# Product 0 of stage one as seven sub-products, taken one batch ahead, from the second expert on

## The chip, the cores and the metric

The kernel runs on 1 core of a Trainium2 chip. The metric is device time in microseconds (us), the median of three runs of one launch. The engines are TensorE (PE; its weight loads are listed as PEld), VectorE (DVE), ScalarE (ACT), GpSimd (POOL) and SyncE (SP), which issues the DMAs.

## The reference, cut to what matters

A block-sparse attention (4 batches, 8 heads, 768 tokens) makes x of 3072 tokens by 512. Then comes a mixture of 8 experts, where every expert sees every token:

```
for e in range(E):                      # 8 experts
    h = np.maximum(x @ w1[e], 0.0)      # 3072x512 @ 512x1024
    ye = h @ w2[e]                      # 3072x1024 @ 1024x512
    out += P[:, e:e + 1] * ye           # P from w_gate, balanced over rows and columns
```

The change is in `x @ w1[e]`.

## The kernel before

After the attention the experts take most of the time: 32 batches i (8 experts e by 4 batches b of 768 tokens, e, b = divmod(i, 4)). Both matrix products of a batch are made with one level of Winograd's scheme: 7 products of half-size blocks in place of 8. Every fp32 operand is held as a high and a low fp16 part, so one product is three matmuls (high by high, high by low, low by high) for each 128 rows of the contraction.

Stage one (`stage1(i, qi)`, line 1376) goes through four quarters qi of 128 of the 512 hidden columns of a half. Each quarter has 7 products (0, 1, 5, 6, 3, 4, 2) of 6 matmuls, 128x384 each, into one PSUM bank of the pool `ps_h` (4 banks). Product 0 goes by ACT into an fp32 tile a1 of the pool `upool` (8 tiles of tag u); the others are added by DVE (`comb`, line 1397). Sums, ReLU and the split of h into high and low parts follow on ACT, DVE and POOL. Stage two (`stage2(i, p)`, line 1496) has 7 products by 3 token blocks, each a step of 12 matmuls, 128x256, into a bank of `ps_y`; DVE adds it into the fp32 accumulator acc (line 1541).

The main loop over i runs stage two of batch i beside stage one of batch i+1: LEAD = 3 steps of stage two first, then 28 steps of stage one with the other 18 of stage two dealt evenly between them. `Slots` (line 1161) keeps queues of deferred work for DVE, ACT and POOL (splits of h, splits of the next expert's weights, late work of the attention, the balance of P), and runs an item when a tally of planned costs says that its engine is not more than 1 us ahead of PE. `slots.need` runs what is still queued of a key. The compiler then orders the instructions of each engine before the launch: among those that its plan takes as ready, the earlier of the program goes first, so the order on an engine may differ from the program's, and is fixed at run time.

The accumulators of all four batches stay in SBUF. `load_x(i)` (line 1371) loads the seven split sums of x of a batch from DRAM (`xd`) into the tiles `xp`, 384 KB each, at the end of the loop before the one that uses them. The weights of the next expert are loaded, scaled, summed and split during batches b = 1 to 3 (`sum_w1`, `split_w1`, line 1268; `queue_split`, line 1236, is one ACT and one DVE instruction of 128x1024; `queue_sum`, line 1250, is on POOL).

Of the kernel before, what the change touches and what calls it, by code (L numbers as in the profile page):

```python
# [20 lines left out]
P = 128  # L21
# [35 lines left out]
def tile_sparse_attention_moe(  # L57
# [28 lines left out]
    CH = NC // 2  # L86
    TH = S // 2
    NP = 7
    CAP = float(NT) / NE

    const = ctx.enter_context(tc.tile_pool(name="const", bufs=1))
# [14 lines left out]

    dram = ctx.enter_context(tc.tile_pool(name="dram", bufs=1, space=bass.MemoryType.DRAM))
    xd = [dram.tile([P, NP, 2, KH, TH], F16, name=f"xd_{b}") for b in range(B)]

    unread = const.tile([P, S], BF16, name="unread")  # L110

# [143 lines left out]

    def load_x1(i, p):
        nc.sync.dma_start(out=xp[p], in_=xd[i % B][:, p])

    def w1_quads(e):
        r = wr[1]  # L260
# [850 lines left out]
    )  # L1111
    sk = mpool("sk", 1)
    upool = mpool("upool", NU)
    hA = mpool("hA", 1)
    hB = mpool("hB", 1)
    big = mpool("big", 1)
# [9 lines left out]
    hfree = [  # L1126
        (hA if n < NHA else hB).tile([P, 2, TH], F16, name=f"h_{n}") for n in range(NHT)
    ]
    accs = {b: big.tile([P, NC, DM], F32, name=f"acc_{b}") for b in range(B // 2)}
    w1ps = {0: w1p}  # L1130
    spares = [big.tile([P, 2, KH, FH], F16, name=f"w1p_{n}") for n in range(3)]
    follows = {}
    bank[0] = lambda nm: ps_h.tile([P, 512], F32, tag="ph", name=nm)
    spread_bank[0] = lambda nm: ps_h.tile([P, 512], F32, tag="ph", name=nm)

    def acc(t):
        return accs[t // NC][:, t % NC]

    def finish_late():
        slots.need(("late", 0, 0))  # L1140
        late.close()
        right = mpool("right", 1, side="right")
        for b in range(B // 2, B):
            accs[b] = right.tile([P, NC, DM], F32, name=f"acc_{b}")

    aside = set()

# [120 lines left out]
    def split_w1(e):  # L1268
        a, s3 = wr["a"], wr["s3"]
        old = w1ps[e - 1]  # L1270
        new = w1ps[e] = {p: spares.pop(0) for p in (0, 1, 6)}

        def one(p, src):
            queue_split(new[p], src, ("w1", e, p))

        one(0, a[0, 0])
        queue_sum(a[0, 0], a[1, 0], a[0, 0], ("w1", e, 5))
# [11 lines left out]
        return dict((  # L1289
            follow(5, a[0, 0], 0), follow(3, a[1, 1], 1),  # L1290
            follow(4, a[1, 0], 5), follow(2, a[0, 1], 6),
        ))
# [36 lines left out]
    def balance():  # L1329
# [33 lines left out]
        for it in range(8):  # L1363
            slots.add(rows, ("balance",), 4, True, dve=1.4, gap=2)
            slots.add(lambda it=it: cols(it), ("balance",), 2, True, dve=0.9, gap=3)

    ov = out.rearrange("(b p c) d -> b c p d", p=P, c=NC)
    hs = {}
    pwe = {}

    def load_x(i):
        b = i % B
        for p in PORDER:
            load_x1(i, p)

    def stage1(i, qi, used=None):
        fs = slice(qi * P, (qi + 1) * P)
# [14 lines left out]

        def fresh(nm):
            return upool.tile([P, TH], F32, tag="u", name=f"{nm}_{i}_{qi}")

        def comb(t, ps, other):
            nc.vector.scalar_tensor_tensor(  # L1397
                out=t, in0=ps, scalar=HDOWN, in1=other, op0=ALU.mult, op1=ALU.add
            )

        def emit(p, src, relu=False, delay=0):
            key = ("h", i, p), i, qi
# [165 lines left out]
    def queue_weight(e):  # L1568
        slots.add(lambda: expert_weight(e), ("pwe", e), 2, True, dve=0.5)

    NI = NE * B
    ORDER2 = (1, 0, 5, 6, 3, 4, 2)
    LEAD = 3

    def run(steps):
        for _ in steps:
# [15 lines left out]
    queue_weight(0)  # L1592

    def products(i):
        e, b = divmod(i, B)
# [19 lines left out]

    for i in range(NI):
        e, b = divmod(i, B)
        nxt = e + 1 < NE
        if i == 2:
            finish_late()  # L1620
        if b == LB2 and nxt:
            for p in range(NP):
                slots.need(("w2", e, p))
        if b == LB1 and nxt:
            slots.need(("scale", 2, e + 1))
            load_w(1, e + 1)
            scale_w(1, e + 1)
            sum_w1(e + 1)
            follows[e + 1] = split_w1(e + 1)
# [5 lines left out]
        n1, n2 = NP * FH // P, NP * CH  # L1635
        for n in range(LEAD):
            next(two)
        done = 0
        for n in range(n1):
            next(one)  # L1640
            want = (n + 1) * (n2 - LEAD) // n1
            for _ in range(want - done):
                next(two)
            done = want
        run(one)
        run(two)
        if i + 2 < NI:
            load_x(i + 2)

# [27 lines left out]
```

## Time and profile before

| what | us |
|---|---|
| median of 3 runs | 2179.38 (2177.88 to 2180.33) |
| the profiled execution, first to last instruction | 2175.5 |
| start of stage two of batch 0, about | 437 |
| one batch from then on, about | 55 |

The page gives the busy share of each engine; the chain of waits says what held up the end; the timeline tells how long after a product its reader was done. A matmul's row holds its pipeline as well, so the spacing of starts, not a row's length, is the rate. Times are counted from the first instruction.

### The profile page before, as it was taken

How to read it: one execution, taken by the hardware profiler on the slowest of the kernel's cores; microseconds unless marked ns; L12 is line 12 of the kernel's file. 1: busy time of each engine (PE TensorE's matmuls, PEld its weight loads, DVE VectorE, ACT ScalarE, POOL GpSimd, SP SyncE). 2: the span in 40 equal slices, each digit the busy share in tenths (PEclk: the TensorE clock that was granted, in tenths of full speed). 3: DMA queues.
4: the chain of work that ended last, by engine and by line, in shares of the span. 5: the costliest groups of instructions: out<-in, count | busy, mean ns of one | idle time of the engine just before them, and what ended most of it. 6: DMA issues, size and time to landing. Idle time of an engine off the chain costs nothing.

```text
span 2175.5 us, 47076 instructions
## 1 busy us (share of the span) xinstructions
PE 2139.2 (98%) x18796; PEld 1590.6 (73%) x18796; DVE 1698.4 (78%) x2982; ACT 1285.5 (59%) x2390; POOL 1439.6 (66%) x1502
## 2 busy tenths in 40 slices
PE   6999999999999999999999999999999999999999
PEld 4777776677777777777777777777777777777777
DVE  8889988777878767877787778777877787778765
ACT  5888888766465656554655455545554555455442
POOL 5667778578557765875586658665866576657553
PEclk9999999999999999999999999999999999999999
DMA  6857795132022112211222121212121212131221
GB/s 172 189 128 176 170 216 140 46 134 66 30 97 89 49 49 90 89 53 52 91 70 72 52 91 55 87 52 91 52 90 52 91 52 90 52 91 59 81 81 52
DMA packets 195632, 192.34 MB, mean 88 GB/s; under 512 B 132412, under 2 KB 150868, under 8 KB 195412
## 3 DMA queue, kind: packets, MB, share of 16 engines
q1 hardware_dynamic: 194848, 189.30, 30.7%
q8 instruction: 147, 2.41, 0.5%
q14 instruction: 73, 0.60, 0.1%
q10 hardware_dynamic: 564, 0.03, 0.0%
HBM read 140.54 MB, written 17.30 MB: 73 GB/s over the span
## 4 chain that ended last, share of the span: by engine, by line
PE 83%; DVE 7%; POOL 5%; ACT 3%; issue 2%; DMA 0%; POOLq 0%; DVEq 0%; ACTq 0%
PE py L1517 37%; PE p L1385 35%; PE u L806 3%; PE t L741 2%; PE t L744 2%; PE m L708 2%; PE m L711 2%; DVE top L717 2%; POOL h L1417 1%; DVE h L1417 1%; ACT h L1406 1%; POOL s L1465 1%; ACT pe L749 1%; DVE vl L617 0%; DVE h L1411 0%
## 5 line engine op out<-in xcount | busy, mean ns | idle before, releaser
L1517 PEld LDWEIGHTS <-h 128*128 128x128 f16 x8064 | 788.4, 98 | 154.2 <-issue 2.5
L1517 PE MATMUL py<-w2p,h 128*128 128x256 f16 x4608 | 564.8, 273 | 1.2 <-ACT acc L1538 0.7
L1417 POOL TENSOR_TENSOR h<-u,h 128x384 f16<-128x384 f32 x128 | 133.0, 1039 | 517.7 <-ACT h L1406 517.7
L1517 PE MATMUL py<-vault,h 128*128 128x256 f16 x3456 | 413.5, 273 | 1.0 <-DVE h L1411 0.7
L1541 DVE SCALAR_TENSOR_TENSOR acc<-py,spare,acc 128x256 f32<-128x256 f32 (+1 forms) x588 | 299.7, 514 | 87.1 <-PE py L1517 82.0
L1406 ACT ACTIVATE h<-c 128x384 f16<-128x384 f32 x256 | 132.9, 519 | 335.7 <-DVE c L1397 281.6
L1385 PEld LDWEIGHTS <-attic 128*128 128x128 f16 x2208 | 215.8, 98 | 120.8 <-issue 1.2
L1385 PEld LDWEIGHTS <-arena 128*128 128x128 f16 x1728 | 168.8, 98 | 91.8 <-issue 0.9
L1417 DVE TENSOR_TENSOR h<-s,h 128x384 f16<-128x384 f32 x128 | 114.6, 895 | 142.3 <-ACT h L1406 142.2
L1397 DVE SCALAR_TENSOR_TENSOR a<-p,a 128x384 f32<-128x384 f32 x384 | 211.4, 550 | 15.8 <-PE p L1385 4.0
L1385 PE MATMUL p<-attic 128*128 128x384 f16 x1152 | 212.0, 326 | 0.0
L1385 PE MATMUL p<-arena 128*128 128x384 f16 x1152 | 210.8, 326 | 0.4 <-DVE c L1397 0.2
L717 DVE TENSOR_REDUCE top<-m 128x1 f32<-128x768 f32 x192 | 182.1, 951 | 32.0 <-PE m L711 30.7
L749 ACT ACTIVATE pe<-t,qk 128x768 int32<-128x768 f32 x192 | 172.6, 901 | 58.2 <-PE t L744 47.4
L1385 PEld LDWEIGHTS <-w1p 128*128 128x128 f16 x1440 | 140.7, 98 | 77.5 <-issue 0.4
L1385 PE MATMUL p<-arena,attic 128*128 128x384 f16 x1056 | 194.8, 326 | 0.0
L1261 POOL TENSOR_TENSOR c<-c,r 128x384 f32<-128x384 f32 x128 | 159.8, 1248 | 10.0
L1406 ACT ACTIVATE h<-r 128x384 f16<-128x384 f32 x256 | 129.6, 516 | 60.2 <-POOL r L1261 58.6
L1261 POOL TENSOR_TENSOR r<-s,r 128x384 f32<-128x384 f32 x128 | 157.4, 1230 | 10.1
L1385 PE MATMUL p<-arena,w1p 128*128 128x384 f16 x864 | 161.3, 326 | 0.0
L763 POOL TENSOR_SCALAR pl<-pe 128x768 f16<-128x768 uint16 x126 | 109.4, 870 | 67.3 <-ACT pe L749 66.7
L1465 POOL TENSOR_TENSOR s<-a,u 128x384 f32<-128x384 f32 x128 | 133.4, 1042 | 29.9 <-ACT a L1462 29.0
(211 smaller groups left out, 4327.1 us busy)
## 6 DMA issues: line engine op xcount, KB each, us to landing
arena<-xd SPq DMA_DIRECT2D x128, 384.0 KB, 3.4
attic<-xd SPq DMA_DIRECT2D x96, 384.0 KB, 3.5
r<-in_moe_w_dram SPq DMA_DIRECT2D x14, 2048.0 KB, 8.6
arena<-in_q_dram SPq DMA_DIRECT2D x16, 384.0 KB, 4.3
arena<-in_k_dram SPq DMA_DIRECT2D x16, 384.0 KB, 4.6
vault<-in_v_dram SPq DMA_DIRECT2D x16, 384.0 KB, 5.5
xd<-xs_t SPq DMA_DIRECT2D x16, 384.0 KB, 3.6
out_dram<-acc SPq DMA_DIRECT2D x48, 128.0 KB, 1.7
```

Of the source, the lines that this page charges most:

```text
L717: nc.vector.tensor_reduce(out=tops[n][:, c : c + 1], in_=sc[:, :S], axis=AX.X, op=ALU.max)
L749: nc.scalar.activation(pe, sc[:, :S], AF.Exp, bias=EXP_SHIFT, scale=qk[n // 2][3])
L763: nc.gpsimd.tensor_scalar(lo, low, FINE, 1.0, ALU.mult, ALU.mult)
L806: nc.tensor.matmul(uv[:, c, :n], lhsT=l[:, c * P : (c + 1) * P], rhs=w[:, h, kc, :n], start=(kc == 0 and c == 0 and m == 0), stop=(kc == N ...
L1261: nc.gpsimd.tensor_tensor(out=out, in0=x, in1=y, op=ALU.subtract)
L1385: nc.tensor.matmul(ps, lhsT=w1ps[i // B][p][:, l, kc, fs], rhs=xp[p][:, r, kc], start=(kc == 0 and m == 0), stop=(kc == KH - 1 and m == 2),)
L1397: nc.vector.scalar_tensor_tensor(out=t, in0=ps, scalar=HDOWN, in1=other, op0=ALU.mult, op1=ALU.add)
L1406: nc.scalar.activation(h[:, 0], src, AF.Relu if relu else AF.Copy)
L1417: eng.tensor_tensor(out=h[:, 1], in0=src, in1=h[:, 0], op=ALU.subtract)
L1465: nc.gpsimd.tensor_tensor(out=s1, in0=a1, in1=u3, op=ALU.add)
L1517: nc.tensor.matmul(py, lhsT=hs[i, p, kc][:, l, tsl], rhs=w2p[p][:, r, kc], start=(old is None and kc == 0 and m == 0), stop=(kc == KF // 2 ...
L1541: nc.vector.scalar_tensor_tensor(out=dst, in0=src, scalar=c, in1=dst, op0=ALU.mult, op1=ALU.add)
```

## The change

From batch 4 (`FIRST_FINE = B`) on, product 0 is no longer made by `stage1` in four quarters. A generator `fine(i)` makes all of it with a second level of the scheme: 7 sub-products of 6 matmuls, 128x192 each. A second-level operand of the weights (`finer["w"]`, from four POOL instructions and one split for each expert) and of x (`finer["x"]`, from DRAM `xfd`, made once for each b by `queue_fine_x` during the first expert) are new. Three banks of `ps_h` are used one after the other: bx for sub-products 0 and 1, by for 5, 6 and 3, bz for 4 and 2. A later sub-product is added in PSUM onto the earlier one of its bank, after ACT (bx) or DVE has read that. The result stands in two tiles `pair` of a new pool `apool` (3 tiles), and `stage1` takes its a1 from there, so a quarter has six products. `fine(i+1)` runs during `stage1(i)`: after each of its steps from the third quarter on (`QFINE = 2`) comes one sub-product, so seven sub-products in all. `fine(4)` has no batch before it and runs at the head of its own.

To make room, two accumulators stay in SBUF in place of four: each batch's accumulator goes to DRAM after its stage two (`keep_acc`), and the next batch's comes back in the loop before it is needed (`fetch_acc`, after 8 of 24 steps of stage one). `load_fine` takes the load of `xp[0]` out of `load_x` and adds that of `finer["x"]`. LEAD goes from 3 to 4. `split_w1(1)` moves from the loop of batch 1 to that of batch 2. The core of the diff:

```diff
+    def fine(i, used=None):
...
+        def product(p, ps, first):
+            for f in range(2):
+                for m, (l, r) in enumerate(((0, 0), (0, 1), (1, 0))):
+                    nc.tensor.matmul(
+                        ps[:, f * TQ : (f + 1) * TQ],
+                        lhsT=ws[p][:, l, f * P : (f + 1) * P], rhs=xs[p][:, r],
+                        start=first and f == 0 and m == 0, stop=f == 1 and m == 2,
+                        skip_group_check=True,
+                    )
...
+        bx, t0 = bank_("fx"), fresh("t0")
+        product(0, bx, True)
+        nc.scalar.activation(t0, two(bx), AF.Copy, scale=HDOWN)
+        tick(0, 1)
+        yield
+        product(1, bx, False)
+        nc.scalar.activation(part(0, 0), two(bx), AF.Copy, scale=HDOWN)
+        tick(0, 1)
+        yield
+        by, t5 = bank_("fy"), fresh("t5")
+        product(5, by, True)
+        comb(t5, two(by), t0)
...
+        t6 = fresh("t6")
+        product(6, by, False)
+        comb(t6, two(by), t0)
...
+        product(3, by, False)
+        comb(part(1, 0), two(by), t0)
...
+        bz = bank_("fz")
+        product(4, bz, True)
+        comb(part(1, 1), two(bz), t6)
...
+        product(2, bz, False)
+        comb(part(0, 1), two(bz), t5)
+        if used:
+            used[0]()
+            used[FINE_P]()
+        if i + 1 < NI:
+            load_fine(i + 1)
...
-        a1 = fresh("a1")
-        nc.scalar.activation(a1, product(0), AF.Copy, scale=HDOWN)
-        tick(0, 1)
-        yield
+        if i < FIRST_FINE:
...
+        else:
+            a1 = pairs[i][qi // 2][:, qi % 2]
...
+        ahead = fine(i + 1, swap(i + 1)) if FIRST_FINE <= i < NI - 1 else None
         for qi in range(FH // P):
-            swap = qi == FH // P - 1 and b == B - 1 and e + 1 < NE
-            yield from stage1(i, qi, follows[e + 1] if swap else None)
+            for _ in stage1(i, qi, swap(i) if qi == FH // P - 1 else None):
+                yield 2
+                if ahead and qi >= QFINE and next(ahead, "end") != "end":
+                    yield 0
...
+        if i < 3:
+            queue_fine_x(i)
         if i == 2:
             finish_late()
+            queue_fine_x(3)
+            follows[1] = split_w1(1)
...
+        for step in one:
+            spent += step
+            if spent >= FETCH and i + 1 >= B and (i + 1) not in fetched:
+                fetched.add(i + 1)
+                fetch_acc((i + 1) % B)
+            want = spent * (n2 - LEAD) // span
             for _ in range(want - done):
                 next(two)
             done = want
...
         if i + 2 < NI:
             load_x(i + 2)
+        if e + 1 < NE:
+            keep_acc(b)
```

`queue_fine_x(b)` is one load of 384 KB, two POOL instructions of 128x384 and four of 128x192, one of ACT and one of DVE of 128x768, and a store of 384 KB. It and the weight steps go into the queue that `Slots` serves before the one of the balance.

## Rows read from the trace of the kernel before

**Rows 1.** The page: span, busy time of the engines, and the granted clock of PE in 40 slices.

```profile
span 2175.5 us, 47076 instructions
...
PE 2139.2 (98%) x18796; PEld 1590.6 (73%) x18796; DVE 1698.4 (78%) x2982; ACT 1285.5 (59%) x2390; POOL 1439.6 (66%) x1502
...
PEclk9999999999999999999999999999999999999999
```

**Rows 2.** The chain of waits over the whole span, in order of time: start, length, what, how many instructions.

```profile
894.26 3.90 PE p L1385 x24
...
1044.87 5.24 PE py L1517 x48
...
2088.53 5.24 PE py L1517 x48
```

**Rows 3.** All waits of PE for another engine from 715 us to the end: total, times, longest.

```profile
PE py L1517 <- DVE acc L1541: 0.5, 2, 0.2
```

**Rows 4.** The timeline of PE, then of its weight loads, in the attention, where small matmuls of 65 and 64 columns stand in a row.

```profile
300.70 0.19 PE L806 MATMUL u<-vq,pl 128*128 128x65 f16 x1
...
300.94 0.19 PE L806 MATMUL u<-vh,pe 128*128 128x65 f16 x1
300.98 0.38 PE L741 MATMUL t<-qt,kt 128*128 128x512 f16 x1
...
300.77 0.10 PEld L806 LDWEIGHTS <-pl 128*128 128x128 f16 x1
300.80 0.13 PEld L806 LDWEIGHTS <-pe 128*128 128x128 f16 x2
```

**Rows 5.** Groups of weight loads, each form apart: busy, mean ns of one, idle before.

```profile
L1517 PEld LDWEIGHTS <-h 128*128 128x128 f16 x8064 | 788.4, 98 | 154.2 <-issue 2.5 <-DVE h L1411 1.4 <-DVE h L1417 0.7
```

**Rows 6.** Groups of ACT, DVE and POOL by line, 770 to 2140 us: the read of product 0, a `comb`, a weight split's low half, a sum of weights.

```profile
L1432 ACT ACTIVATE a<-p 128x384 f32<-128x384 f32 x100 | 47.9, 479 | 31.8 <-PE p L1385 31.8
...
L1397 DVE SCALAR_TENSOR_TENSOR a<-p,a 128x384 f32<-128x384 f32 x300 | 165.2, 551 | 12.8 <-PE p L1385 2.8
...
L1243 DVE SCALAR_TENSOR_TENSOR w1p<-r,sw,w1p 128x1024 f16<-128x1024 f32 x10 | 15.7, 1567 | 0.0
...
L1254 POOL TENSOR_TENSOR t<-r 128x256 f32<-128x256 f32 x24 | 17.0, 728 | 0.0
```

**Rows 7.** Busy time by stretches of 55 us, about one batch each: PE, PEld, DVE, ACT, POOL, each with its count, then granted clock, DMA share, GB/s. The first is the loop of batch 2 (e = 0), the others are, nearly, the loops of batches b = 3, 0, 1, 2.

```profile
550.00:605.00 55.00, 53.30 (x410) 39.54 (x408) 47.44 (x115) 28.35 (x58) 29.38 (x28) 1.00 0.12 38
...
1045.00:1100.00 55.00, 55.00 (x424) 41.27 (x423) 41.35 (x82) 31.71 (x69) 34.87 (x34) 1.00 0.29 90
1100.00:1155.00 55.00, 54.76 (x418) 40.69 (x417) 44.65 (x69) 27.58 (x52) 39.69 (x39) 1.00 0.27 86
1155.00:1210.00 55.00, 55.00 (x424) 41.23 (x422) 42.76 (x78) 32.41 (x69) 42.45 (x36) 1.00 0.18 53
1210.00:1265.00 55.00, 55.00 (x424) 41.27 (x423) 39.78 (x67) 26.77 (x51) 29.41 (x28) 1.00 0.18 52
```

**Rows 8.** Timelines of a calm quarter: PE at products 0 and 1 and the ACT read of product 0; in another quarter PE at product 3 and its `comb` on DVE.

```profile
1075.39 2.11 PE L1385 MATMUL p<-arena 128*128 128x384 f16 x12
...
1076.56 0.49 ACT L1432 ACTIVATE a<-p 128x384 f32<-128x384 f32 x1 [0.85 <-PE p L1385]
...
1015.03 1.14 PE L1385 MATMUL p<-attic,w1p 128*128 128x384 f16 x6
...
1016.21 0.56 DVE L1397 SCALAR_TENSOR_TENSOR c<-p,u 128x384 f32<-128x384 f32 x1 [0.22 <-PE p L1385]
```

**Rows 9.** Timelines of a loaded quarter, the third of a batch with b = 1 (run in the loop of the batch with b = 0): PE at product 5; on DVE a weight split and later that product's `comb`; then PE at product 0 of the fourth quarter (its last two matmuls lie behind the stretch asked for) and its read on ACT.

```profile
1353.56 1.14 PE L1385 MATMUL p<-arena 128*128 128x384 f16 x6
...
1355.20 2.02 DVE L1243 SCALAR_TENSOR_TENSOR w2p<-r,sw,w2p 128x1024 f16<-128x1024 f32 x1
...
1359.60 0.54 DVE L1397 SCALAR_TENSOR_TENSOR a<-p,a 128x384 f32<-128x384 f32 x1
...
1362.47 0.81 PE L1385 MATMUL p<-arena,w1p 128*128 128x384 f16 x4
...
1365.26 0.47 ACT L1432 ACTIVATE a<-p 128x384 f32<-128x384 f32 x1
```

**Rows 10.** The chain of waits, 1325 to 1365 us, in the first half of the same loop.

```profile
1333.80 3.90 PE p L1385 x24
1337.70 0.33 PE py L1517 x3
1338.03 2.92 PE p L1385 x18
```

**Rows 11.** The end of the attention's work for x in the loop of batch 1: PE and the other engines in a stretch of 10 us (columns as in group 7); then DVE and ACT on a 128x768 part of x, and POOL on one of 128x384 (ns: least, median, most).

```profile
510.00:520.00 10.00, 7.72 (x61) 5.67 (x60) 7.12 (x15) 5.98 (x14) 9.76 (x9) 1.00 0.11 41
...
L406 DVE TENSOR_TENSOR xs_t<-xf,xs_t x4: 952/1352/1818, 490.2 to 513.2; 128x768 f16<-128x768 f32 x4
...
L416 POOL TENSOR_TENSOR xf<-xf x8: 991/994/1314, 486.4 to 503.9; 128x384 f32<-128x384 f32 x8
```

**Rows 12.** DMA: issues by line (KB each, median us to landing), and a stretch at the highest rate of the experts (columns as in group 7).

```profile
arena<-xd SPq DMA_DIRECT2D x128, 384.0 KB, 3.4
...
r<-in_moe_w_dram SPq DMA_DIRECT2D x14, 2048.0 KB, 8.6
...
600.00:606.00 6.00, 6.00 (x48) 4.46 (x46) 5.76 (x11) 3.00 (x5) 1.96 (x3) 1.00 0.88 300
```

More of the change, by code (lines that the diff above doesn't have):

```diff
@@ L108, in tile_sparse_attention_moe @@
     xd = [dram.tile([P, NP, 2, KH, TH], F16, name=f"xd_{b}") for b in range(B)]
+    xfd = [dram.tile([P, 2, 4, TQ], F16, name=f"xfd_{b}") for b in range(B)]
+    accd = [dram.tile([P, NC, DM], F32, name=f"accd_{b}") for b in range(B)]
     unread = const.tile([P, S], BF16, name="unread")
@@ L1128, in tile_sparse_attention_moe @@
     ]
-    accs = {b: big.tile([P, NC, DM], F32, name=f"acc_{b}") for b in range(B // 2)}
+    accs = [big.tile([P, NC, DM], F32, name=f"acc_{b}") for b in range(2)]
     w1ps = {0: w1p}
-    spares = [big.tile([P, 2, KH, FH], F16, name=f"w1p_{n}") for n in range(3)]
+    spares = []
+    finer = {}
     follows = {}
@@ L1136, in acc, with keep_acc, fetch_acc @@
     def acc(t):
-        return accs[t // NC][:, t % NC]
+        return accs[t // NC % 2][:, t % NC]
+    def keep_acc(b):
+        nc.sync.dma_start(out=accd[b], in_=accs[b % 2])
+    def fetch_acc(b):
+        nc.sync.dma_start(out=accs[b % 2], in_=accd[b])
     def finish_late():
@@ L1142, in finish_late @@
         right = mpool("right", 1, side="right")
-        for b in range(B // 2, B):
-            accs[b] = right.tile([P, NC, DM], F32, name=f"acc_{b}")
+        spares.extend(
+            right.tile([P, 2, KH, FH], F16, name=f"w1p_{n}") for n in range(3)
+        )
+        finer["sum"] = right.tile([P, 4, FQ], F32, name="w1f_sum")
+        finer["w"] = right.tile([P, 2, 4, FQ], F16, name="w1f")
+        finer["x"] = right.tile([P, 2, 4, TQ], F16, name="xpf")
     aside = set()
@@ L1276, in split_w1, with split_finer @@
         one(0, a[0, 0])
+        for out_, x, y, op in fine_w(finer["sum"], a[0, 0]):
+            slots.add(
+                lambda out_=out_, x=x, y=y, op=op: Pinned.gpsimd.tensor_tensor(
+                    out=out_, in0=x, in1=y, op=op
+                ),
+                ("w1", e, FINE_P), 1, True, pool=0.8,
+            )
+        def split_finer():
+            queue_split(finer["w"], finer["sum"], ("w1", e, FINE_P))
+        if e == 1:
+            split_finer()
         queue_sum(a[0, 0], a[1, 0], a[0, 0], ("w1", e, 5))
@@ L1429, in tick @@
             slots.tick(0.976, 0.55 * n, 0.5 * m)
-        a1 = fresh("a1")
-        nc.scalar.activation(a1, product(0), AF.Copy, scale=HDOWN)
-        tick(0, 1)
-        yield
+        if i < FIRST_FINE:
+            a1 = fresh("a1")
+            nc.scalar.activation(a1, product(0), AF.Copy, scale=HDOWN)
+            tick(0, 1)
+            yield
+        else:
+            a1 = pairs[i][qi // 2][:, qi % 2]
         r11 = fresh("r11")
@@ L1569, in queue_weight @@
         slots.add(lambda: expert_weight(e), ("pwe", e), 2, True, dve=0.5)
-    NI = NE * B
+    FETCH = 16
+    QFINE = 2
+    fetched = set()
     ORDER2 = (1, 0, 5, 6, 3, 4, 2)
-    LEAD = 3
+    LEAD = 4
     def run(steps):
@@ L1628, in tile_sparse_attention_moe @@
             sum_w1(e + 1)
-            follows[e + 1] = split_w1(e + 1)
+            if e:
+                follows[e + 1] = split_w1(e + 1)
         two = outputs(i)
@@ L1634, in tile_sparse_attention_moe @@
         one = products(i + 1)
-        n1, n2 = NP * FH // P, NP * CH
+        n2 = NP * CH
+        span = 2 * (NP * FH // P)
+        if i + 1 >= FIRST_FINE:
+            span += 3 * NP * (i + 1 == FIRST_FINE) - 2 * (FH // P)
         for n in range(LEAD):
             next(two)
[L1638 to L1641, printed above, removed]
+        done, spent = 0, 0
+        for step in one:
[4 more added lines that the diff above has]
+            want = spent * (n2 - LEAD) // span
             for _ in range(want - done):
@@ L1644, in tile_sparse_attention_moe @@
             done = want
-        run(one)
+        assert spent == span, (i, spent, span)
         run(two)
```

129 lines of the change are left out of this document (122 added, 7 removed).

## The prediction, made before the changed kernel was run

> **What bounds the kernel now.** I read four views, in this order. First the page: PE is busy for 98% of the span at a granted clock that stands at 9 tenths or more, in the upper of its two levels (2.4 GHz), in every slice; no other engine is over 78% [rows 1]. Then the chain of waits, behind the attention: it runs over PE alone, and equal places of it lie (2088.53 - 1044.87) / 19 = 54.93 us apart [rows 2]. A row of 24 matmuls of 384 columns takes 3.90 us there (162.5 ns each) and one of 48 of 256 columns 5.24 us (109.2 ns each) [rows 2]. A batch has 168 of the first and 252 of the second: 27.3 + 27.5 = 54.8 us, so the period is filled by streaming columns. Third, PE's waits: 0.5 us in all from 715 us on [rows 3]. So only fewer columns on PE can make a batch shorter, and every new wait of PE makes it longer. Last, the timelines of a quarter: how long after a product its reader has left the bank. That doesn't matter now, because each product has a fresh bank of four; it is what the change leans on.
>
> **The columns saved.** The two spacings differ by 53.3 ns for 128 columns, 0.416 ns a column, so 192 columns should take 109.2 - 64 x 0.416 = 82.5 ns. The 42 matmuls of `fine` are then 3.47 us in place of 24 x 162.5 = 3.90, a gain of 0.435 us a batch, and 28 batches give 12.2 us. All of it lies on the path.
>
> This needs each matmul's own weight load to fit in 82.5 ns. A load's row is 98 ns long [rows 5], but loads overlap one another: nine matmuls of 65 and 64 columns, each with its load, start within 300.98 - 300.70 = 0.28 us, 31 ns apart, and two loads in a row begin 30 ns apart [rows 4]. Loads don't set the pace at 82.5. The Trainium skill ("TensorE: Matmul & The Clock Gate", section "LDWEIGHTS (loading the stationary operand)") gives a load as columns / 1.2 ns, which for 128 is 107 ns; if loads went one by one at that, `fine` would be 4.48 us, 0.58 more than product 0 takes today, and the change a loss of 16 us. The trace of the small matmuls doesn't agree that loads go one by one.
>
> **The chain in PSUM.** This is the added wait. Sub-product 1 may only be added onto bx when ACT has read sub-product 0; 6 and 3 onto by, and 2 onto bz, when DVE has read the one before. PE issues in a fixed order, so behind a late sub-product stands all of PE. The cover is what PE does in between. With 17 steps of stage two dealt over 24 of stage one, a step follows the 13th, 15th, 16th, 17th and 19th product but not the 14th and 18th. So between 0 and 1 lies one product (0.975 us), and between 5 and 6, 6 and 3, 4 and 2 a product and a step of stage two (2.29 us). Now the readers. In a calm quarter ACT is done 1077.05 - 1076.37 = 0.68 us after the product's last column, and DVE 1016.77 - 1016.01 = 0.76 us [rows 8]: both are inside the cover, no wait. In a loaded quarter ACT takes 1365.73 - 1363.45 = 2.28 us and DVE 1360.14 - 1354.54 = 5.60 us, a weight split of 2.02 us being among what stands ahead [rows 9]. In the program's order that is a wait of 1.3 us at bx and 3.3 us at by. So the cost is between 0 and 4.6 us a batch; a gain is excluded, since a wait gives PE nothing.
>
> I take 0.1 us on average, near the lower end, for one reason. The order on PE is not the program's where a reader is late: in a loaded loop four products stand in a row, then 3 matmuls of stage two, then three products more [rows 10], where the even deal would have a step after every one or two. The plan had moved ready work ahead, and PE still waited for only 0.5 us in 1460 [rows 3]. A late sub-product will be passed in the same way; what is left is where plan and chip differ. Twenty-seven batches make 2.7 us.
>
> The banks go with it: one of four is held by the chain, so three are left to stage one while DVE is 5.6 us late [rows 9]. The `upool` tiles also turn over faster, seven instead of five in the third quarter. Both lie in the same range of 0 to 4.6.
>
> **Load on the other engines.** DVE gets five `comb`s of 0.55 us a batch and one split of 1.57 us for each expert [rows 6]; the fullest stretch goes from 44.65 us to at most 48.9 [rows 7], of 54.5. ACT loses two reads of 0.48 us a batch [rows 6]. POOL gets four sums of 0.73 us for each expert [rows 6] on 42.45 us at most [rows 7]. None becomes the bound, and the work is hidden under PE; if DVE were full, each further us on it would be one of the batch.
>
> **The accumulators' trips.** Each loop adds 1.57 MB out, as much back and 0.39 MB for `finer["x"]`: 65 GB/s on 52 to 90 [rows 7]. A stretch of 300 GB/s left PE busy for all of its 6.00 us [rows 12], so traffic itself costs nothing. By the 2 MB load of 8.6 us [rows 12] a trip is about 6.5 us, both are over some 25 us into the loop, or soon after the 8th of 24 steps, and the accumulator is needed at 54. On SP's queue, `fetch_acc` waits for `keep_acc`, and that for the last DVE add of the batch before; behind them stand `load_fine` in the fourth quarter, the x loads of the loop's end and the weight loads at the loop's start, none needed within those 13 us. Taken at 0; if a weight load came 13 us late, the queue of splits would come so much later, which has a loop of room.
>
> **Once.** `fine(4)` runs with nothing of stage one between. The dealing leaves 0 and 1, and 6 and 3, back to back: two waits of 0.68 to 0.76 us [rows 8] and some signalling, 0 to 1.6 us; I take 1.0. Its `xp[0]` is issued behind the last product's tile and lands 3.4 us later [rows 12]; five steps of stage two (6.5 us) cover that. LEAD = 4 moves one step whose inputs are long there: 0.
>
> **The first expert.** Four runs of `queue_fine_x` add about 4 x (2 x 0.99 + 4 x 0.6) = 18 us to POOL, the 0.6 being an estimate from 0.99 for 384 columns, and 4 x 1.35 = 5.4 us to DVE [rows 11]. In the loop of batch 1, PE lost 2.3 us of 10 beside a full POOL [rows 11]. `split_w1(1)` leaves that loop (three splits, 4.7 us of DVE) for the next, where DVE has 47.44 of 55 [rows 7]; with two of the new parts (2.7), the new split (1.6) and those 4.7 it comes to 56.4 and must push some balancing on. So between -2.3 us (the old wait goes) and +5 us (1.4 us of DVE over the loop, and POOL's 18 us partly uncovered); I take +1.0, as the balance waits in the last queue and isn't needed until batch 4.
>
> **Sum.** -12.2 + 2.7 + 1.0 + 1.0 = -7.5 us. The span is 2175.5 us, so 2168.0; the median stands 3.9 us over the span, which I keep: 2172 us.
>
> **Rivals.** (a) The chain in PSUM takes the gain back: slower. For it speak the 5.6 us of lateness against 2.29 of cover [rows 9], and that four banks were just enough for it; against it, that PE's order bends [rows 10]. It decides from 0.435 us of new wait a batch. Kept to the program's order, the loaded loop would lose 3.3 us at by, the next (42.76 us of DVE [rows 7]) perhaps half, the other two 0.1 each: 5.1 us for an expert, 36 us for seven, 2205 us. If passing ahead saves half, 18 us: 2179.4 - 12.2 + 18 + 2 = 2187. I price it at 2187, chance 0.15. (b) The middle: waits of about 0.3 us a batch, 8 us: 2177, no difference that can be told. For it speaks that ACT, between 0 and 1, has only 0.3 us to spare in the calm case; chance 0.22. (c) Loads go one by one at their 98 ns [rows 5]: 42 x 98 = 4.12 us, 0.22 more than before, 6 us in all and the 4.7 of the other terms: 2190, against the 31 ns of [rows 4]; chance 0.03. It is the case in which the change doesn't do what it says. By the rule of the Trainium skill quoted above ("TensorE: Matmul & The Clock Gate", section "LDWEIGHTS (loading the stationary operand)"), with its 16 us, it would be 2200.
>
> **Chances.** Forecast 0.60, (a) 0.15, (b) 0.22, (c) 0.03. A measurement of this kernel tells about 0.2% (4.4 us) from no change, that is 2175.0 and 2183.7: faster 0.60, same 0.22, slower 0.18. The forecast's own range is 2165 (no chain waits, the old wait of the first expert gone) to 2175. For 8 in 10 it reaches over (b) to the half-saved case of (a): 2166 to 2187.
>
> **What would show it.** Right: the sub-products' matmuls 82 to 83 ns apart; equal places of the chain 54.5 us apart from the second expert on; PE's waits behind 715 us under 5 us; `fetch_acc` landed before the middle of a loop. Wrong: waits of PE named for ACT at sub-product 1 or for DVE at 6, 3 and 2, above 0.4 us a batch, first in the loops with b = 0 and 1; PE idle between 490 and 660 us by more than now, with POOL or DVE named; starts 98 ns apart.

## The result, and the profile after

The changed kernel takes 2190.56 us (median of 5 runs, 2189.34 to 2193.12), the kernel before in the same comparison 2179.04 us (2177.88 to 2180.33): a ratio of 1.0057, interval 1.0044 to 1.0069. It is slower by half a per cent. The forecast was 2172, its range 2166 to 2187.

The page of the changed kernel, which answers to [rows 1]:

```profile
span 2188.7 us, 48783 instructions
...
PE 2133.6 (97%) x19300; PEld 1620.4 (74%) x19300; DVE 1814.4 (83%) x3133; ACT 1279.3 (58%) x2345; POOL 1491.9 (68%) x1554
```

PE is busy for 5.6 us less than before, in a span that is 13.2 us longer: what was lost is waiting, and in a few places a lower clock. The chain of waits where the sub-products of the fourth expert's first batch are made, and further equal places of it over the whole span, answer to [rows 2]:

```profile
1042.60 0.49 PE fx L1512 x6
...
1046.36 0.17 PE fy L1512 x2
1046.52 0.49 PE fx L1512 x6
1047.02 0.33 PE fy L1512 x4
...
1065.96 6.55 PE py L1709 x60
```

```profile
1120.39 6.55 PE py L1709 x60
1175.83 6.55 PE py L1709 x60
...
1941.63 6.55 PE py L1709 x60
```

Six matmuls of a sub-product take 0.49 us, 82 ns each. At 1046.36 PE makes two matmuls of a sub-product of one bank, then the six of fx, then the other four: the plan had moved ready work between them. Equal places lie 1120.39 - 1065.96 = 54.43 us apart (54.87 before), and 55.44 us in the one loop of four that has the waits. Those waits, from 740 us to the end, answer to [rows 3]:

```profile
PE fx L1512 <- ACT t L1534: 5.4, 6, 0.9
PE py L1709 <- DVE acc L1733: 0.5, 1, 0.5
```

So the steady part is faster than before, as forecast, though by less (see below). To see where the loss lies I cut PE's instructions at the start of stage two of each batch: loop k begins with the first py matmul of batch k, that is with every 252nd of these matmuls in the order of their starts (in the kernel before, loop 0 begins at 417 us by this, not at the 437 or so of the table of times). The table is counted from the traces in that way; "idle" is the part of 400 us to loop 5 in which no matmul ran.

| start of loop (us) | before | changed kernel | e1 | e11 | e15 |
|---|---|---|---|---|---|
| 0 | 417.02 | 420.32 | 416.60 | 417.25 | 417.58 |
| 1 | 491.11 | 504.63 | 492.60 | 492.96 | 491.69 |
| 2 | 549.02 | 560.23 | 550.26 | 549.75 | 548.78 |
| 3 | 606.81 | 617.73 | 610.44 | 606.54 | 608.73 |
| 5 | 716.82 | 738.46 | 730.75 | 728.82 | 724.97 |
| end of the span | 2175.5 | 2188.7 | 2181.0 | 2176.2 | 2172.9 |
| idle, 400 us to loop 5 | 5.9 | 18.8 | 15.5 | 10.9 | 9.7 |

At loop 5 the changed kernel is 738.46 - 716.82 = 21.6 us late; from there to the end it takes 1450.2 us against 1458.7, a gain of 8.5. Of the 21.6 us, 2.6 is work brought forward: 3 x 42 x 82.5 ns of sub-products (batches 4 to 6) less two product 0s of 3.90 us. **The whole loss, 19.0 us, was made before loop 5, in the loops of the first expert and at the entry to the second.** Loop 0 begins 3.3 us later and is 10.2 us longer than before, loops 1 and 2 together are 2.6 us shorter, and loops 3 and 4 lose 8.1 us beside the work brought forward. The trace of the kernel before is of one of its shorter executions (its span lies 3.9 us under the median of its runs, that of the changed kernel 1.9 us), so about 2 of the 19.0 us may lie between executions and not between kernels.

The largest piece stands in loop 0. The same three stretches of 10 us in the kernel before, and then in the changed one (columns as in [rows 7]):

```profile
420.00:430.00 10.00, 9.88 (x66) 6.07 (x65) 9.36 (x14) 6.62 (x13) 8.32 (x8) 1.00 0.00 0
430.00:440.00 10.00, 9.64 (x62) 5.80 (x62) 8.36 (x14) 7.26 (x16) 8.64 (x9) 1.00 0.79 238
440.00:450.00 10.00, 9.47 (x71) 6.62 (x70) 8.34 (x12) 7.09 (x16) 9.43 (x9) 1.00 0.10 40
```

```profile
420.00:430.00 10.00, 9.25 (x63) 5.96 (x62) 8.35 (x11) 6.04 (x13) 10.00 (x11) 1.00 0.13 38
430.00:440.00 10.00, 7.97 (x42) 4.59 (x42) 8.99 (x13) 5.58 (x11) 10.00 (x10) 0.83 0.28 86
440.00:450.00 10.00, 5.75 (x26) 2.80 (x25) 6.90 (x11) 5.91 (x12) 9.84 (x10) 0.83 0.63 202
```

POOL is full, PE makes 26 matmuls where it made 71, and the granted clock falls to 0.83 in two of the stretches. It is low while PE works: in the two stretches of 4 us with the lowest values, from 432 and from 448 us on (0.61 and 0.76), PE counts as busy for all of the time. So 2 x 0.17 x 10 = 3.4 us of the loss are the clock, and not a wait. What fills POOL is the preparation of x, on POOL's timeline from 405 us on:

```profile
406.25 1.78 POOL L1454 TENSOR_TENSOR fx<-fsrc 128x384 f32<-128x384 f16 x2
...
418.74 1.78 POOL L1454 TENSOR_TENSOR fx<-fsrc 128x384 f32<-128x384 f16 x2 [0.64 <-DMA fsrc<-xd]
...
433.11 3.07 POOL L1454 TENSOR_TENSOR fx<-fsrc 128x384 f32<-128x384 f16 x2
```

Three of the four runs of `queue_fine_x` start before 436 us; in the program the third is queued in the loop of batch 2, which begins at 560. (The fourth, queued there too, starts at 482.) The compiler, which orders each engine's instructions before the launch, had moved them ahead. The chain of waits shows how that reaches PE:

```profile
437.46 1.10 POOL fsum L1460 x2
...
441.62 0.60 POOL fsum L1460
...
442.24 0.85 ACT fst L1464
...
443.12 0.66 DVE fst L1468
...
444.76 1.26 DVE h L1606
446.02 0.48 DVE r L1484
...
446.54 3.77 PE p L1579 x12
```

And the timeline of DVE at that place:

```profile
439.37 0.88 DVE L1606 TENSOR_TENSOR h<-a,h 128x384 f16<-128x384 f32 x1
443.12 1.72 DVE L1468 TENSOR_TENSOR fst<-fsum,fst 128x768 f16<-128x768 f32 x1 [2.87 <-ACT fst L1464]
```

DVE stands idle for 2.87 us, its next instruction being the low half of an x that is loaded again more than 200 us later (at 676.7), and behind it stands the `comb` (r) for which PE waits 4.3 us by the list of its waits. The Trainium skill ("Perfetto Trace Analysis", section "Tensor Engine Instruction (MATMUL, LD_WEIGHTS)") says that DVE, ACT and GpSimd take their instructions strictly first in, first out; this row agrees for DVE.

### The profile page after: what moved, and what is told of

Read it like the earlier page. It is cut to its first block, busy times and chain, and to the rows that moved or that the text cites. A ratio compares the mean times of both kernels' runs of the same rounds, so it can differ in the third digit from the quotient of the medians.

```text
span 2188.7 us, 48783 instructions
## 1 busy us (share of the span) xinstructions
PE 2133.6 (97%) x19300; PEld 1620.4 (74%) x19300; DVE 1814.4 (83%) x3133; ACT 1279.3 (58%) x2345; POOL 1491.9 (68%) x1554
## 4 chain that ended last, share of the span: by engine, by line
PE 62%; DVE 14%; POOL 13%; issue 5%; ACT 5%; DMA 1%; POOLq 0%; DVEq 0%; ACTq 0%; SPq 0%
PE py L1709 27%; PE p L1579 21%; PE u L834 3%; POOL h L1606 2%; POOL s L1657 2%; DVE h L1606 2%; PE t L769 2%; PE t L772 2%; DVE top L745 2%; PE m L736 2%; PE m L739 2%; POOL r L1294 2%; PE fy L1512 1%; DVE acc L1733 1%; ACT h L1595 1%
## 5 line engine op out<-in xcount | busy, mean ns | idle before, releaser
L1709 PE MATMUL py<-w2p,h 128*128 128x256 f16 x4608 | 571.5, 273 | 0.2 <-DVE w2p L1283 0.2
L1606 POOL TENSOR_TENSOR h<-u,h 128x384 f16<-128x384 f32 x128 | 126.7, 990 | 457.6 <-ACT h L1595 455.5
L1579 PEld LDWEIGHTS <-attic 128*128 128x128 f16 x2016 | 197.0, 98 | 114.7 <-issue 11.6
L1579 PE MATMUL p<-attic 128*128 128x384 f16 x1152 | 217.8, 329 | 8.2 <-DVE r L1484 6.5
L1579 PEld LDWEIGHTS <-arena 128*128 128x128 f16 x1440 | 139.9, 98 | 75.9 <-issue 3.8
L1657 POOL TENSOR_TENSOR s<-a,u 128x384 f32<-128x384 f32 x128 | 151.4, 1183 | 45.3 <-ACT a L1654 45.3
L1579 PEld LDWEIGHTS <-w1p 128*128 128x128 f16 x1248 | 121.2, 98 | 63.0 <-DMA arena<-xd 0.7
L1595 ACT ACTIVATE h<-s 128x384 f16<-128x384 f32 x128 | 66.9, 523 | 165.2 <-POOL s L1657 154.5
L1579 PE MATMUL p<-arena 128*128 128x384 f16 x864 | 162.0, 327 | 0.8 <-DVE a L1484 0.7
L1579 PE MATMUL p<-arena,attic 128*128 128x384 f16 x864 | 162.5, 326 | 0.0
```

The lines of the kernel that those rows point to most:

```text
L1579: nc.tensor.matmul(ps, lhsT=w1ps[i // B][p][:, l, kc, fs], rhs=xp[p][:, r, kc], start=(kc == 0 and m == 0), stop=(kc == KH - 1 and m == 2),)
L1595: nc.scalar.activation(h[:, 0], src, AF.Relu if relu else AF.Copy)
L1606: eng.tensor_tensor(out=h[:, 1], in0=src, in1=h[:, 0], op=ALU.subtract)
L1657: nc.gpsimd.tensor_tensor(out=s1, in0=a1, in1=u3, op=ALU.add)
L1709: nc.tensor.matmul(py, lhsT=hs[i, p, kc][:, l, tsl], rhs=w2p[p][:, r, kc], start=(old is None and kc == 0 and m == 0), stop=(kc == KF // 2 ...
```

## The experiments

Medians of different batches of runs differ by up to 2 us for the same kernel (2177.4 to 2179.5 for the kernel before), so each ratio is to the kernel before in the same batch; where single pieces are taken apart I use the starts of the loops in the profiled executions.

**e1_pinned.** `Slots.run` keeps a few kinds of deferred steps from going ahead of their place; the new kind is added to them.

```diff
-if key[0] in ("scale", "w1", "w2", "late", "balance"):
+if key[0] in ("scale", "w1", "w2", "late", "balance", "fine_x"):
```

> The changed kernel, with the steps of queue_fine_x kept from going ahead of their place in the program, as the weight steps are. Theory: the compiler put three of the four runs of queue_fine_x at 406 to 444 us, beside a POOL that was full for 30 us; this cost 13 of the 11.5 + 12 us between forecast and result, so the time falls to 2178 to 2181. Rival 1 (the added POOL work costs wherever it stands): 2187 to 2191. Rival 2 (the accumulators' trips to DRAM are the cost): 2188 to 2192.

Measured: 2184.83 us, 1.0027 (1.0015 to 1.0038). The first `fx` instruction now starts at 451.0, loop 0 takes 76.0 us instead of 84.3, and loop 5 starts 7.7 us earlier; 3.4 of these are the clock, which is not low anywhere before the end of this trace. The cause is real, but 14 us at loop 5 stay (2.6 of them the work brought forward), and the time is 4 us over what was expected.

**e2_no_sums.** The changed kernel without `queue_fine_x`; `finer["x"]` is loaded from another product's split.

> The changed kernel without queue_fine_x: finer x is loaded from another product's split, so the sub-products 3 to 6 have wrong operands of the right size. Theory: the 13 us of the first loop go, and a little of the rest of the first expert: 2174 to 2179. Rival 1: the same here, but then the pinned kernel stays at 2187 or more. Rival 2: 2188 to 2192.

Measured: 2183.69 us, 1.0025 (1.0014 to 1.0035), loop 5 at 731.21, as in e1_pinned. Missed: with the lead at four the preparation, once in its place, is not what is left, or not by itself.

**e3_trips_only.** The kernel before with two accumulators and their trips through DRAM, nothing else.

> The kernel before, with two accumulators and their trips to DRAM and back, and nothing else of the change. Theory: the traffic is hidden, 2178 to 2181. Rival 2: 2186 or more.

Measured: 2180.03 us (median of ten runs, one of which took 8010 us), 1.0006 (0.9997 to 1.0016), loop 5 at 716.77. The trips cost 1.9 us of span, 1.5 of it in six waits of py for acc, in the loops with b = 0. The issues of the changed kernel (KB each, median us to landing) are as estimated:

```profile
accd<-acc SPq DMA_DIRECT2D x28, 1536.0 KB, 5.8
acc<-accd SPq DMA_DIRECT2D x28, 1536.0 KB, 6.5
```

**e4_third_expert.** As e1_pinned, with sub-products from batch 8 on and the preparation in the second expert (`FIRST_FINE = 2 * B`).

> The changed kernel with the sub-products from batch 8 on in place of batch 4, the steps of queue_fine_x in the second expert and kept from going ahead. Theory: the first expert has no new load, so no idle time there; 24 x 0.435 = 10.4 us saved, less 0.9 us of waits in one loop of each expert (5 us) and 1 to 2 us at the start: 2172 to 2177. Rival 1 (the preparation costs wherever it stands): 2184 or more. Rival 2: 2186 or more.

Measured: 2186.11 us, 1.0034 (1.0021 to 1.0047). Missed. Loops 2 to 4, which hold no sub-product now, and the preparation of one batch in loop 4 alone, still took 173.5 us against 167.8 before (loop 4 by itself 59.32 against 55.15): something else of the change was costing time there.

**e5_split_back.** As e1_pinned, with `split_w1(1)` back in loop 1 and all of the preparation and the new weight split in loop 2.

> The pinned kernel with split_w1(1) back in the loop of batch 1 (its three tiles stand on the left, apool on the right), and all four runs of queue_fine_x and the new weight split of expert 1 in the loop of batch 2. For expert 1 the four weight sums of the second level read an operand that is already summed, so its product 0 is wrong at the same work. Theory A (split_w1(1) in the loop of batch 2, where DVE is full, makes the rest of the loss in the loops of batches 2 to 4, with 10 us over its work): most of it goes, 2174 to 2178. Theory B (fine(4) at the head of its batch makes it, by its chain and by the weight splits that it forces): 2180 to 2184. Theory C (queue_fine_x makes it): 2182 or more.

Measured: 2190.46 us, 1.0060 (1.0040 to 1.0081), from two runs. Loops 2 to 4 took 181.3 us, with a mean granted clock of 0.97 in loops 3 and 4, against 180.5 in e1_pinned: they are no shorter without the three splits. But all of the preparation was moved into loop 2 at the same time, so the run doesn't separate theories A and C. Loop 1, where the splits stand again, now beside four leading steps, took 62.67 us against 57.66; e10_lead_four below shows the same there (62.73).

**e6_no_head.** As e1_pinned, without `fine(4)`: the two tiles that it fills are set to zero.

> The pinned kernel without fine(4): batch 4's product 0 is left at zero by four short memsets, so 3.5 us of PE work and everything that this run at the head waits for are left out. Theory B: the loops of batches 3 and 4 fall by 3.5 us of work and by 4 us or more of waits, 2174 to 2177. Theory A: by the work alone or a little more, 2178 to 2181.

Measured: 2180.07 us, 1.0015 (1.0004 to 1.0025). Loop 5 starts 2.95 us earlier than in e1_pinned, less than the 3.47 us of the matmuls left out. The granted clock is low in this trace at 608 to 616 us (0.87 and 0.71, which is (0.13 + 0.29) x 4 = 1.7 us) and not in that of e1_pinned; with these 1.7 us added it would be 1.2 us more than the work. The 4 us of waits at the head aren't there: theory B fell.

**e8_deal.** As e1_pinned; no sub-product after the 14th, 18th and 21st product, so that each has a step of stage two before the next of its bank.

```diff
-if ahead and qi >= QFINE and next(ahead, "end") != "end":
+if ahead and qi >= QFINE and made not in (14, 18, 21) and next(ahead, "end") != "end":
```

> The pinned kernel with no sub-product after the 14th, 18th and 21st step of stage one, so that a step of stage two lies between any two sub-products of a bank. Theory: the 0.9 us wait of PE for ACT at sub-product 1, in one loop of each expert, goes and no other comes: 5 us less than the pinned kernel, 2176 to 2180. Rival (the wait comes from ACT being late by more than a step of stage two, or the later sub-products make new ones): within 2 us of the pinned kernel, 2181 to 2185.

Measured: 2184.49 us, 1.0037 (1.0023 to 1.0052). The wait of fx for ACT is gone, and in its place stand six of p for c (2.7 us) and six for a (2.2 us). No gain: the rival was right.

**e9_split_moved.** e3_trips_only, with `split_w1(1)` in loop 2 as in the changed kernel.

> The kernel before with two accumulators, their trips, and split_w1(1) in the loop of batch 2; no sub-products. Theory A: 4 to 7 us over the run with the trips alone, in the loops of batches 2 to 4, 2183 to 2187. Theory B: within 2 us of it, 2178 to 2182.

Measured: 2180.61 us, 1.0014 (1.0004 to 1.0025); loop 5 at 719.16, 2.4 us behind e3_trips_only. The time is in theory B's range. 1.7 of the 2.4 us are a lower clock behind a pause that the kernel before has as well (rows in the last section), so the moved splits cost between 0.7 and 2.4 us: at most a part.

**e10_lead_four, e11_lead_three.** One number each: the kernel before with four leading steps of stage two (the diff below), and e1_pinned with three (the other way round).

```diff
-    LEAD = 3
+    LEAD = 4
```

> The kernel before with one number changed: four steps of stage two instead of three stand ahead of stage one in each loop. Theory E (the fourth leading step meets activations that are not combined yet, in the loops of the first expert): 2180 to 2183, with new PE waits of py for h or acc in the loops that begin at 549 to 662, and none later. Rival (the lead is free, and the start's loss comes of the order in which the queue of deferred steps hands out work): 2177 to 2179.

> The changed kernel with the preparation of x pinned (as in e1_pinned), and three leading steps of stage two as before the change. Theory E: 3 to 4 us under e1_pinned, 2180 to 2182, loops 2 to 4 (the starts of stage two of batches 2 to 5) shorter by as much. Theory D (the splits of expert 1's first-stage weights stand behind other steps in the queue, so that the load of its second-stage weights begins at 630 where it began at 617, and the balancing and the splits of w2 are pressed into loops 3 and 4): 2184 to 2186, and the load still at about 630.

Measured: e10_lead_four 2181.79 us, 1.0014 (1.0005 to 1.0022), loop 5 at 722.61, 5.8 us late, of which the loops after it give 1.9 back; e11_lead_three 2178.35 us, 0.9998 (0.9989 to 1.0007), 6.5 us under e1_pinned by the medians and 4.8 by the spans. The total of e10_lead_four bears theory E out and that of e11_lead_three goes beyond it, by 1.7 us; the places don't. In e10_lead_four the price lies in loop 1 (62.73 us against 57.91, 1.7 of it by the clock, which is 0.79 and 0.78 in the two stretches of 4 us from 540 us on), earlier than expected and mostly in waits of stage one; loops 2 to 4 of e11_lead_three are shorter by 1.4 us (179.1 against 180.5) and not by 3 to 4. PE's waits in e10_lead_four, 415 to 740 us:

```profile
PE p L1385 <- DVE a L1397: 3.2, 2, 2.4
PE cs L1354 <- DVE spare L1348: 2.2, 2, 1.9
PE py L1517 <- DVE acc L1541: 1.3, 1, 1.3
```

What theory E had not said: of the 4.8 us between e1_pinned and e11_lead_three only 1.9 come before loop 5. The rest is in the steady loops. From 740 us on e11_lead_three has these waits:

```profile
PE py L1709 <- DVE vault L1283: 1.8, 6, 0.3
PE p L1579 <- DVE a L1484: 1.5, 6, 0.3
```

The six waits of fx for ACT (5.5 us in e1_pinned) are gone. The dealing gives the reason. After the n-th product of stage one, n x 17 / 24 steps of stage two (rounded down) have been dealt with four leading, n x 18 / 24 with three. Between the 13th and the 14th that is 9 and 9 with four: sub-products 0 and 1 have one product between them. With three it is 9 and 10: a step of 1.31 us more, and the ACT read is covered. In e8_deal, where a step was put there in another way, this wait is gone too.

**e12_split_first.** e11_lead_three, with `split_w1(1)` queued ahead of the preparation of batches 2 and 3.

> As e11_lead_three, and in the third loop the splits of expert 1's first-stage weights are queued ahead of the preparation of x for batches 2 and 3, not behind it. Theory D: the splits are at about 560 (591 to 614 in e1_pinned), the load of the second-stage weights at about 620, and the time 4 to 8 us under e11_lead_three: 2174 to 2178. Rival (the work of the start does not fit into loops 2 to 4 in any order, since VectorE and ACT are filled with the combining of the sub-products as well): within 2 us of e11_lead_three, the waits only moved.

Measured: 2179.61 us, 1.0005 (0.9996 to 1.0014). The splits came at 558 to 566 us and the load of the second-stage weights began at 619.3 (625.5 in e11_lead_three), yet loop 5 began at 727.91, 0.9 us earlier. Theory D fell: the order of the queue isn't it.

**e13_lead_alone.** The changed kernel with three leading steps, not pinned.

> The changed kernel with three leading steps and nothing else undone (the preparation of x is not pinned). If the two causes add up: the result less 6.5 us, 2183 to 2185, with POOL still full at 420 to 450. Rival (with three leading steps the order of the instructions falls out otherwise, and nothing is moved ahead, or more is): outside 2181 to 2187.

Measured: 2185.87 us, 1.0026 (1.0016 to 1.0036), POOL 10.00, 10.00 and 9.84 of 10 us in the three stretches from 420 on. That is 0.9 us over the range expected. By the spans of the profiled executions the lead alone gives 4.7 us, the pin alone 7.7 and both together 12.5 (by the ratios 6.8, 6.5 and 12.9): the two causes add up.

**e14_third_lead_three.** e4_third_expert with three leading steps.

> e4_third_expert (sub-products from the third expert on, preparation pinned in the second) with three leading steps. Theory (the loss belongs to the first expert's loops, which were full already, and to the lead): the start costs at most 3 us in loops 6 to 8 beyond the work done ahead, and the time is 2174 to 2177. Rival (the start costs some 7 us wherever it is put, because loop 7 runs two batches of sub-products in one loop): 2179 to 2182, and loops 6 to 8 take 173 to 175 us together, against 164.7 in the kernel before.

Measured: 2177.63 us, 0.9992 (0.9983 to 1.0001), 8.5 us under e4_third_expert. Loops 6 to 8 take 172.7 us, 8.0 over before, of which the brought-forward work is 2.6. Between the two expectations: the start costs about 5 us there too, but loops 4 and 5, with one batch prepared in each, take 55.14 and 54.87 us, as before (55.15 and 54.87). Loop 6, with two, takes 57.16.

**e15_no_sums_lead_three.** e2_no_sums with three leading steps.

> e2_no_sums (nothing prepared for x, so that the second-level operand of x is made of other numbers) with three leading steps. Theory (the preparation on POOL, ACT and DVE holds up loops 1 to 3): 4 to 6 us under e11_lead_three, 2172 to 2175. Rival (the preparation fits into idle time once it is pinned): 2177 to 2179, boundary of loop 5 at 727 to 729 as in e11_lead_three.

Measured: 2174.40 us, 0.9978 (0.9968 to 0.9987), 4.0 us under e11_lead_three; loop 5 starts 3.9 us earlier. The preparation does cost 4 us before loop 5. With four leading steps no such gain was seen (e2_no_sums against e1_pinned); why isn't shown.

**e16_lead_two.** e12_split_first with two leading steps.

> e12_split_first with two leading steps. Theory (a leading step too many is what delays the combining of stage one): at or just under e12_split_first, 2177 to 2180. Rival (with two, the first products of stage two wait for activations or splits that are not there): 2181 to 2190, with PE waits of py at the start of every loop.

Measured: 2207.11 us, 1.0123 (1.0109 to 1.0137), 27 us over e12_split_first and far over both ranges. The side was the rival's, the wait was not the one it named: six waits of p for a (14.1 us), one in each loop with b = 0, and a lower clock behind each (last section). Of two, three and four leading steps, three is best.

**e17_calm_start.** e14_third_lead_three, with `split_w1(1)` back in loop 1 (its memory is free there because the pool `apool` is made only later) and the four batches of x prepared in loops 3, 4, 5 and 6.

```diff
-        if FIRST_FINE - B <= i < FIRST_FINE - 1:
-            queue_fine_x(i % B)
-        if i == FIRST_FINE - 2:
-            queue_fine_x(3)
+        if FIRST_FINE - B - 1 <= i < FIRST_FINE - 1:
+            queue_fine_x(i - (FIRST_FINE - B - 1))
```

> Sub-products from the third expert on, three leading steps (e14_third_lead_three), with two things moved: the splits of expert 1's first-stage weights are back in the second loop as in the kernel before, and the four batches of x are prepared in loops 3, 4, 5 and 6, one in each, instead of 4, 5, 6 and 6. Theory (these steps cost nothing in a loop whose engines have room): loops 3 to 6 take 54.8 to 55.5 us each, boundary of loop 5 within 0.7 us of the kernel before, 4 to 5 us under e14_third_lead_three: 2172 to 2174. Rival (the preparation costs about 1 us for each batch wherever it runs): 2176 to 2178, with loops 3 to 6 at 55.5 to 57 us.

Measured: 2175.85 us, 0.9984 (0.9975 to 0.9993): faster than both kernels, by 3.3 us than before, and 2 us short of the theory. Loops 3 to 6 take 55.16, 56.01, 54.87 and 56.11 us, in all 2.5 over before: 0.6 us for each batch prepared, between theory and rival. Loop 5 starts at 719.16, 2.3 us late and not within 0.7; that lateness is made in loop 1 (59.58 us against 57.91), before any preparation of x.

## Why the prediction was wrong

**What held.** The columns saved: 82 ns a matmul, 0.44 us a loop, as in the sum; so loads don't go one by one, and rival (c) is out. The chain in PSUM: 5.9 us of waits from 740 us on, with 0.5 before, twice the term of 2.7, whose range went to 4.6 a batch; PE's order did bend (1046.36 to 1047.02), and 5.4 of the 5.9 stand at the place that rival (b) named, sub-product 1 behind ACT. Rival (a), the only slower one besides (c), would have made the steady part slower than before; it gained 8.5 us, 5.9 without the 2.6 brought forward, against 9.5 in the sum. The trips: 0 in the sum, 1.9 us of span in e3_trips_only, where the comparison of times can't tell them from 0. The run of `fine(4)`: 1.0 in the sum, about 1 us in e6_no_head once the clock is taken out.

**The step that failed: "The first expert".** It stood at +1.0, between -2.3 and +5; with "Once" it was 2.0, and 19.0 was measured. (The miss of 18.6 us is these 17.0, the 3.6 that the steady part fell short, and -2.0, because span and median lie 1.9 us apart in the changed kernel and not 3.9.) It fails in three ways, in order of size. First, the estimate took the preparation to run in the loop in which it is queued. The compiler moved three runs of it ahead, to 406 to 444 us, beside a POOL that was 83 to 94% busy already; 7.7 us at loop 5 (e1_pinned), 3.4 of them by the lower clock behind the pauses of PE. The prediction quoted the same freedom of the plan as a reason why PE would wait little [rows 10], and didn't ask which of the new instructions that freedom applied to. Its sign for this step, PE idle between 490 and 660 us, looked past the place: loops 1 and 2 (504.6 to 617.7) are 2.6 us shorter than before, and the loss stands ahead of them and behind them.

Second, it summed DVE and POOL over a whole loop (56.4 of 55 us, 18 us on POOL) and took what fits in the sum as hidden. In its place in the program the preparation still costs 3.9 us (loop 5 of e11_lead_three against e15_no_sums_lead_three). One way in which it costs time without filling a loop is shown above: its instruction on DVE waits for ACT, and what stands behind it waits too. DVE was idle for this 4.5 us in the changed kernel and 5.3 us in e1_pinned. But in e11_lead_three, from which the 3.9 us are read, it was 0.2 us:

```profile
L1468 DVE TENSOR_TENSOR fst<-fsum,fst x4: 953/1079/1283, 459.9 to 582.5; 128x768 f16<-128x768 f32 x4
...
  ACT fst L1464: 0.2, 1
```

There the cost comes out later, in loop 3 (65.16 us against 59.68), behind the last instruction of the preparation. The chain of waits of e11_lead_three at the start of loop 3 shows the place, where PE waits for 3.1 us:

```profile
607.01 0.41 DVE acc L1733
607.42 1.88 DVE w1p L1283
609.30 0.41 DVE spare L1402
609.70 0.47 DVE c L1484
...
611.82 4.23 PE py L1709 x19
```

A split of the next expert's weights and a step of the balance stand on DVE ahead of the `comb` from which the h of the waiting step of stage two is made; a lower clock behind the pause takes 2.5 us more (last section). With the preparation the splits of w1 run at 580 to 609 us, without it (e15_no_sums_lead_three) at 558 to 573. That the preparation pushes them there, and that this is the cost, isn't shown: with the splits first (e12_split_first) loop 5 begins only 0.9 us earlier.

Third, the moved splits, priced at nothing by themselves, cost 0.7 to 2.4 us (e9_split_moved).

**The second step that failed: "LEAD = 4 moves one step whose inputs are long there: 0".** It cost 1.9 us before loop 5 and 2.8 after it (spans of e1_pinned and e11_lead_three), 2.9 us by itself in the kernel before (e10_lead_four). Inputs that were late are a small part of it (py waited 0.5 us for h in the first loops of e10_lead_four); in the steady loops what it changed was the deal. Why it costs time in the first loops, without sub-products too, is not shown beyond the waits listed. The prediction had counted from that very deal that only one product lies between sub-products 0 and 1, and did not ask what three leading steps would give.

Added up at loop 5, in one row of runs that each undo one thing more: 7.7 (moved ahead, e1_pinned) + 1.9 (lead, e11_lead_three) + 3.9 (preparation in its place, e15_no_sums_lead_three) = 13.5 of the 19.0 us. The lower clock is in these pieces, and not in the same measure: 3.4 us in the changed kernel, none in e1_pinned, 2.5 us in e11_lead_three, none in e15_no_sums_lead_three. Of the 5.5 us that are left, the moved splits are 0.7 to 2.4. **What stays open** is the rest, 3 to 5 us. About 2 us may be the short execution in which the kernel before was traced. In loops 3 and 4 of e15_no_sums_lead_three PE waits 1.4 us for DVE at by and 0.5 us for ACT at bx, the chain in PSUM of the first sub-products. The start costs about 5 us in e14_third_lead_three as well, outside the first expert, of which two batches prepared in one loop are about 2; neither `fine(4)` (e6_no_head) nor the order of the queue (e12_split_first) accounts for the rest.

## What to carry to other kernels

Work that is "off the path" and early is not free: ask of each deferred instruction how far ahead the scheduler may move it, and what stands behind it on its in-order engine while it waits for its own input. A loop's sum of busy time bounds the cost of such work only from below; put it where the loop before shows all engines with room, one portion to a loop. And when a constant of the interleaving changes along with the work, count the deal for both values: here one leading step cost more than half of what the change was to gain (4.8 of 7.5 us). Before a difference of a few us between two traces is given to a change, compare the granted clock in both.

## What the runs showed of the hardware

A lower clock can make a short pause of PE dearer. Stretches of 4 us in e11_lead_three around the pause above (columns as in [rows 7]):

```profile
604.00:608.00 4.00, 3.68 (x31) 2.77 (x29) 3.93 (x8) 2.22 (x3) 4.00 (x4) 1.00 0.71 203
608.00:612.00 4.00, 0.79 (x3) 0.26 (x4) 3.90 (x7) 1.63 (x4) 0.22 (x1) 0.77 0.03 11
612.00:616.00 4.00, 4.00 (x20) 2.87 (x19) 2.56 (x5) 1.91 (x4) 3.64 (x3) 0.50 0.59 246
616.00:620.00 4.00, 4.00 (x37) 3.49 (x35) 3.19 (x5) 3.48 (x9) 3.84 (x4) 0.88 0.60 200
```

PE is busy 0.79 of 4 us; the granted clock goes from 1.00, its upper level (2.4 GHz), to 0.77, then 0.50, its lower level (1.2 GHz), for all of the next 4 us, in which PE counts as fully busy and issues 20 matmuls, where 31 were issued in 3.68 us before the pause. At these rates the two stretches behind the pause lose 0.50 x 4 + 0.12 x 4 = 2.5 us on top of the 3.2 us in which PE stood still. A pause of 2.4 us in each of six loops of e16_lead_two came with a mean clock of 0.971 over each of those loops of 58.7 us. None of the pauses up to 0.9 us in the loops of the changed kernel behind 740 us was followed by a lower clock.

It does not follow every pause of the same length. In the kernel before and in e9_split_moved PE waits at the same place, for 1.6 us and then for 0.7; the first two rows are of the kernel before, the other two of e9_split_moved:

```profile
516.00:520.00 4.00, 1.72 (x14) 1.01 (x12) 3.51 (x12) 2.06 (x5) 4.00 (x4) 1.00 0.20 79
520.00:524.00 4.00, 4.00 (x29) 2.68 (x28) 3.06 (x7) 2.86 (x5) 3.12 (x3) 1.00 0.00 0
```

```profile
516.00:520.00 4.00, 1.69 (x11) 0.97 (x9) 3.36 (x12) 1.99 (x5) 4.00 (x4) 0.86 0.18 71
520.00:524.00 4.00, 4.00 (x20) 2.13 (x19) 1.75 (x6) 1.35 (x3) 3.02 (x3) 0.72 0.00 0
```

In e9_split_moved PE makes 20 matmuls in the second of these stretches where it made 29: (0.14 + 0.28) x 4 = 1.7 us more, for the same wait. So a difference of 2 or 3 us between two traces can be one such place, and is not yet one of the kernels.
